# A new order of the beginning of an mLSTM with two feed-forward layers: scores among the broadcasts, and q and k of the third and fourth unit ahead of the first and second weight

## The chip, the cores and the metric

The kernel runs on one core of a Trainium2 chip. The metric is the device time of one execution in microseconds. The core's engines work side by side, each through its own list of instructions in order: TensorE (PE; its weight loads are shown as PEld), VectorE (DVE), ScalarE (ACT), GpSimd (POOL) and SyncE (SP), which here issues every transfer between DRAM and the core's memory. They wait for each other by semaphores.

## What is computed

A recurrent attention over 768 steps (batch 2, 8 heads, head dimension 40), and two feed-forward layers over its 1,536 tokens of width 320:

```python
for t in range(S):
    m_new = np.maximum(f_gate[:, :, t] + m, i_gate[:, :, t])
    f_stab = np.exp(f_gate[:, :, t] + m - m_new)
    i_stab = np.exp(i_gate[:, :, t] - m_new)
    m = m_new
    C = f_stab[:, :, None, None] * C + i_stab[:, :, None, None] * np.einsum('bhd,bhe->bhde', vt, kt)
    n = f_stab[:, :, None] * n + i_stab[:, :, None] * kt
    h_tilde = np.einsum('bhde,bhe->bhd', C, qt)
    denom = np.maximum(np.abs(np.einsum('bhd,bhd->bh', n, qt)[:, :, None]), 1.0)
    y[:, :, t] = h_tilde / denom / (1.0 + np.exp(-o_gate[:, :, t]))
h = np.maximum(np.maximum(x @ w1, x @ w2), x @ w3)     # 320 -> 768
x = h @ w_out                                          # 768 -> 320
h = x @ w_in                                           # 320 -> 2048
out = (h * np.tanh(softplus(h))) @ w_out2              # 2048 -> 320
```

## The kernel before

The recurrence is done in chunks of 128 steps. Six chunks times two batches make 12 units, numbered u0 to u11 in the code (u = 2 x chunk + batch); the "third and fourth unit" of the title are u2 and u3. Within a unit a step depends on the others through a 128 x 128 matrix of decays for each head, and on earlier chunks through a state. The first feed-forward layer runs in three blocks of 512 tokens (four units each), so its products (line 578) begin when u0 to u3 are through. Everything after that is products on TensorE, with the other engines converting weights and evicting results.

No scheduler decides the order. A text, PLAN, is read word by word, and each word calls a small function that records its instructions; each engine then runs what was recorded for it, in that order:

```python
def follow(plan):
    for word in plan.split():
        name, _, rest = word.partition(":")
        args, _, tags = rest.partition("@")
        act[name](*[int(a) if a.lstrip("-").isdigit() else a for a in args.split(",") if a], *[t for t in tags.split(",") if t])
```

The words of the beginning that are spoken of below, u being a unit:

- `first:n` loads the gates of the first chunk (fi0), of the others (fir), the identity (ident, into idt) or a mask. `ln:u` loads na (v, k and the output gate of a unit, 484 KB), `lq:u` q and k (line 300, two transfers), `l3:u` q in another layout, `lc:u` a broadcast cp, `fet:w,g` weight g of the first layer.
- `ma`, `fa`, `fe`, `fl`, `ia`, `ie` make the decays of the gates on VectorE, ScalarE and GpSimd; `pick` and `eye` make sel and idr from idt on ScalarE (lines 267 and 271).
- `F:u,j` broadcasts a row of decays over 128 partitions by four matmuls with sel (line 339); `D:u,j` scans it into half of the decay matrix dt on VectorE (line 346).
- `S:u` are the scores, q times k, eight matmuls (line 359); `X:u,j` multiplies them with dt on VectorE (line 365).
- `V:u` and `K:u` scale v and k by gates on GpSimd (lines 371, 381); `N:u` is the product of scores and v, with the state's part from u2 on (lines 398, 396); `den`, `sg`, `xn`, `xc` divide and gate; `T:u` transposes the result (line 429); `O`, `C`, `sd` bring the state forward.
- `sc`, `mg`, `rd`, `cut` convert a weight: two passes on ScalarE (lines 503, 504), a merge on VectorE (line 509), a split into two parts.
- `fill:n` are n matmuls on a cleared tile, whose result nobody reads:

```python
def _lq(u):
    for j in range(2):
        nc.sync.dma_start(qks[u % 2][64 * j:64 * j + D], qk2[u, j])
def _fill(n, tag):
    ps = bank(tag, f"fill{len(fills)}")
    fills.append(ps)
    for _ in range(n):
        nc.tensor.matmul(ps, warm[:, 0:P], warm, start=True, stop=True)
```

q and k have two buffers, so `lq:2` writes where u0's were and waits for `S:0`, and `lq:3` for `S:1`. na has two buffers as well; weights are fetched into three. All transfers stand in SP's one list, and SP waits in it: what is listed behind a waiting transfer is not issued.

Of the kernel before, what the change touches and what calls it, by code (L numbers as in the profile page):

```python
# [15 lines left out]
B, H, S, D = 2, 8, 768, 40  # L16
# [12 lines left out]
ZAT = (5, 12, 13)  # L29
LATE = {4: "i7", 6: "p4", 8: "p5", 10: "p6", 12: "p7"}  # L30
PLAN = (
# [882 lines left out]
```

## Time and profile before

| | us |
|---|---|
| three runs, median (lowest to highest) | 382.39 (374.51 to 383.19) |
| the profiled execution | 374.55 |
| its span, first to last instruction | 372.8 |
| TensorE busy in it | 367.4 |
| first products of the feed-forward layer start at | 33.31 |

Times in the rows are counted from the start of the span. A row of a timeline gives start, duration, engine, line, operation, out<-in and the shape, x the number of instructions merged into it, and in brackets the idle time before it with what ended it. A matmul's end is modelled, and some matmul records are missing (one of the 22 fills).

### The profile page before, as it was taken

The page shows a single profiled execution, that of the slowest core. Times are in us where ns is not written, and L with a number is a line of the kernel's source. Part 1 is how long each engine was busy: PE and PEld are TensorE (multiplying, and loading weights), DVE is VectorE, ACT ScalarE, POOL GpSimd, SP SyncE. Part 2 cuts the span into 40 slices and gives each one's busy share as a digit, 9 for nine tenths or more (in the row PEclk, how much of TensorE's full clock was granted, in tenths as well). Part 3 has the DMA queues.
Part 4 walks back from the last instruction along what each step waited for, and adds up shares of the span by engine and source line. Part 5 has one row for each costly group of instructions (what it writes and reads, how often), then busy time and mean ns, then how long its engine had stood idle before and what let it go on. Part 6 is the DMA issues. An engine that isn't in the chain of part 4 may idle for free.

```text
span 372.8 us, 7435 instructions
## 1 busy us (share of the span) xinstructions
PE 367.4 (99%) x2999; PEld 317.2 (85%) x3000; DVE 198.6 (53%) x344; ACT 175.5 (47%) x353; POOL 100.1 (27%) x111
## 2 busy tenths in 40 slices
PE   8999999999999999999999999999999999999996
PEld 4898888888888898888777889989989989989986
DVE  6989999998556853565581745512212112212112
ACT  4887777933413202555644876543333233333231
POOL 6784575755202022311540052330010110000000
PEclk9999999999999999999999999999999999999999
DMA  7879995938590310033220530000200000200001
GB/s 204 270 248 307 355 283 166 267 100 273 192 316 8 105 55 2 18 123 110 103 70 2 223 131 3 3 2 0 72 2 2 2 0 2 72 2 3 2 0 70
DMA packets 15668, 38.80 MB, mean 104 GB/s; under 512 B 1886, under 2 KB 8515, under 8 KB 15635
## 3 DMA queue, kind: packets, MB, share of 16 engines
q1 hardware_dynamic: 15635, 38.34, 31.3%
q8 instruction: 23, 0.38, 0.4%
q14 instruction: 10, 0.08, 0.1%
HBM read 36.29 MB, written 2.04 MB: 103 GB/s over the span
## 4 chain that ended last, share of the span: by engine, by line
PE 90%; DVE 3%; DMA 3%; ACT 1%; issue 1%; SPq 1%; DVEq 0%; ACTq 0%
PE mm L578 24%; PE o L719 23%; PE h L719 22%; PE it L398 4%; PE sc_c L359 2%; PE mz L621 2%; PE mz L620 2%; PE mz L622 2%; PE it L396 2%; DMA qall<-in_qk_dram 2%; PE mz L625 1%; PE mz L626 1%; PE sp L460 1%; DMA idt<-in_ident_dram 1%; PE xp L429 1%
## 5 line engine op out<-in xcount | busy, mean ns | idle before, releaser
L748 DVE TENSOR_TENSOR gl<-g,gh 128x512 fp32r<-128x512 f32 x48 | 34.8, 729 | 102.0 <-ACT g L747 102.0
L719 PE MATMUL o<-wo,gh 64*128 64x320 f32 (+1 forms) x736 | 85.0, 306 | 0.0
L719 PE MATMUL h<-zh,wi 64*128 64x512 f32 x480 | 75.2, 390 | 0.0
L578 PE MATMUL mm<-xh,w 128*128 128x512 f32 x270 | 72.0, 396 | 0.0
L719 PEld LDWEIGHTS o<-wo,gh 64*128 64x128 f32 (+1 forms) x736 | 65.1, 185 | 2.2 <-issue 0.4
L746 ACT ACTIVATE gh<-h 128x512 fp32r<-128x512 f32 x48 | 29.0, 604 | 77.8 <-PE h L719 77.6
L719 PE MATMUL o<-wo,gl 64*128 64x320 f32 (+1 forms) x368 | 59.3, 306 | 0.0
L578 PEld LDWEIGHTS mm<-xh,w 128*128 128x128 f32 x270 | 49.4, 188 | 10.7 <-issue 0.4
L719 PEld LDWEIGHTS h<-zh,wi 64*128 64x128 f32 x480 | 44.1, 185 | 9.3 <-ACT zraw L633 0.5
L719 PE MATMUL h<-zl,wi 64*128 64x512 f32 x240 | 47.3, 391 | 0.0
L578 PE MATMUL mm<-xl,w 128*128 128x512 f32 x162 | 45.7, 390 | 0.1
L578 PEld LDWEIGHTS mm<-xl,w 128*128 128x128 f32 x162 | 30.3, 188 | 6.9 <-issue 0.5
L719 PEld LDWEIGHTS o<-wo,gl 64*128 64x128 f32 (+1 forms) x368 | 36.1, 185 | 0.0
L596 DVE TENSOR_TENSOR zraw<-zraw,mm 128x512 f32<-128x512 f32 x36 | 24.6, 682 | 20.7 <-PE mm L578 19.1
L747 ACT ACTIVATE g<-h 128x512 f32<-128x512 f32 x48 | 29.2, 608 | 0.0
L719 PEld LDWEIGHTS h<-zl,wi 64*128 64x128 f32 x240 | 22.5, 184 | 5.3 <-issue 0.4
L658 POOL TENSOR_TENSOR zl<-zraw,zh 128x512 fp32r<-128x512 f32 x9 | 11.6, 1291 | 54.9 <-ACT zh L652 54.8
L606 POOL TENSOR_TENSOR hl<-zraw,hh 128x512 fp32r<-128x512 f32 x11 | 15.3, 1388 | 39.1 <-DVE hh L152 24.0
L398 PE MATMUL it<-vp,dt 128*128 128x41 f32 x192 | 25.2, 272 | 0.2 <-DVE dt L365 0.2
L398 PEld LDWEIGHTS it<-vp,dt 128*128 128x128 f32 x192 | 24.1, 192 | 0.5 <-DVE dt L365 0.3
L594 ACT ACTIVATE zraw<-mm 128x512 f32<-128x512 f32 x18 | 10.7, 592 | 21.8 <-PE mm L578 21.7
L346 DVE TENSOR_TENSOR_SCAN dt<-dt,eye 128x512 f32<-128x512 f32 x16 | 19.1, 1206 | 0.0
(153 smaller groups left out, 523.0 us busy)
## 6 DMA issues: line engine op xcount, KB each, us to landing
na<-in_nat_dram SPq DMA_DIRECT2D x12, 484.0 KB
raw_w<-in_w_dram SPq DMA_DIRECT2D x9, 640.0 KB
raw_i<-in_wi_dram SPq DMA_DIRECT2D x8, 640.0 KB
raw_p<-in_wo_dram SPq DMA_DIRECT2D x8, 640.0 KB
dt<-dram_f SPq DMA_DIRECT2D x8, 512.0 KB
qall<-in_qk_dram SPq DMA_DIRECT2D x24, 160.0 KB
raw_o<-in_wo_dram SPq DMA_DIRECT2D x3, 640.0 KB
out_dram<-ob SPq DMA_DIRECT2D x12, 160.0 KB
```

What stands on the lines that cost most here:

```text
L346: nc.vector.tensor_tensor_scan(half, *((t["fp", j], idr) if ("fp", j) in t else (half, eyes[0])), 0.0, op0=ALU.mult, op1=ALU.add)
L359: nc.tensor.matmul(scs[h % 2][:, (h // 2) * L:(h // 2 + 1) * L], qk[r:r + 64, 1, h // 2], qk[r:r + 64, 0, h // 2], start=True, stop=True)
L398: nc.tensor.matmul(it[:, h], t["dt"][:, h], vps[u % 2][:, h], start=(c == 0), stop=(c == 0 or h == h1 - 1))
L578: nc.tensor.matmul(ups[blk, m, i], *seq[k], start=(k == 0), stop=(k == 7))
L594: nc.scalar.activation(top(blk, m), ups[blk, m, 0], AF.Copy)
L596: nc.vector.tensor_tensor(top(blk, m), top(blk, m), ups[blk, m, i], op=ALU.max)
L606: engine(dve).tensor_tensor(ls, top(blk, m), h.bitcast(F32), op=ALU.subtract)
L658: nc.gpsimd.tensor_tensor(zl[:, j], zraw[:, j, t0:t0 + tb], zh[:, j].bitcast(F32), op=ALU.subtract)
L719: mm = nc.tensor.matmul(out_, a, r, start=first, stop=last).ins
L746: mark[blk, m] = nc.scalar.activation(gh, ps, AF.Mish)
L747: nc.scalar.activation(g, ps, AF.Mish)
L748: low[blk, m] = nc.vector.tensor_tensor(gl, g, gh.bitcast(F32), op=ALU.subtract)
```

## The change

The first lines of PLAN are written in another order. Nothing else differs: the same functions record the same work, but for ten fills fewer (22 to 12) and two table loads of ScalarE fewer (5 to 3), which follow from the order of exponentials and sigmoids. The first six lines of PLAN are new; from the seventh on the order is the same.

```diff
-    "tables: clear:4 first:0 clear:1 clear:2 clear:0 clear:3 fill:9@m1 first:1 clear:5 ln:0 first:2 lq:0 fet:w,0 ma:0 lq:1 l3:2 fa:0 fill:2@m0 ma:1 fe:0 fill:4@c1 "
...
+    "tables: clear:4 first:0 first:1 clear:1 clear:2 clear:0 clear:3 fill:8@m1 first:2 clear:5 clear:7 clear:6 lq:0 ln:0 ma:0 lq:1 ln:1 fa:0 ma:1 fe:0 "
+    "pick: eye: fa:1 ia:0 fl:0 fe:1 ie:0 F:0,1@m2 fill:2@m1 ma:2 ia:1 F:0,0@c0 ca:1 fl:1 D:0,1 out:1 flp:1 ie:1 F:1,1@m0 D:0,0 S:0@s0,s2 first:3 lq:2 l3:2 fet:w,0 fa:2 "
...
```

On SyncE, the transfers behind those of the gates (fi0, fir): na is v, k and o of a unit, qall q and k, raw_w a weight. Before:

```order
L305 DMA na0_132<-in_nat_dram 128x968
L186 DMA idt_86<-in_ident_dram 128x161
L300 DMA qall_93<-in_qk2_dram 40x1024 x2
L494 DMA raw_w0_137<-in_w13_dram 128x1280
L300 DMA qall_93<-in_qk2_dram 40x1024 x2
L310 DMA q32_143<-in_q3_dram 120x384
L294 DMA dram_c_104<-scr_105 16x128
L295 DMA dram_c_104<-scr_105 1x128
L305 DMA na1_206<-in_nat_dram 128x968
L186 DMA bmt_88<-in_bmask_dram 120x8
L494 DMA raw_w1_224<-in_w13_dram 128x1280
```

and now:

```order
L186 DMA idt_86<-in_ident_dram 128x161
L300 DMA qall_93<-in_qk2_dram 40x1024 x2
L305 DMA na0_139<-in_nat_dram 128x968
L300 DMA qall_93<-in_qk2_dram 40x1024 x2
L305 DMA na1_145<-in_nat_dram 128x968
L294 DMA dram_c_104<-scr_105 16x128
L295 DMA dram_c_104<-scr_105 1x128
L186 DMA bmt_88<-in_bmask_dram 120x8
L300 DMA qall_93<-in_qk2_dram 40x1024 x2
L310 DMA q32_203<-in_q3_dram 120x384
L494 DMA raw_w0_205<-in_w13_dram 128x1280
```

The identity moved ahead of na of u0, na of u1 came forward, and weight 0 moved behind q and k of u2 (the third qall).

Further down the same list, up to the third weight (raw_w2); cp is the broadcast of decays. Before:

```order
L300 DMA qall_93<-in_qk2_dram 40x1024 x2
L305 DMA na2_285<-in_nat_dram 128x968
L310 DMA q33_289<-in_q3_dram 120x384
L300 DMA qall_93<-in_qk2_dram 40x1024 x2
L330 DMA cp3_308<-dram_c_104 40x3x128 x3
L305 DMA na3_366<-in_nat_dram 128x968
L494 DMA raw_w2_372<-in_w13_dram 128x1280
```

and now:

```order
L300 DMA qall_93<-in_qk2_dram 40x1024 x2
L305 DMA na2_268<-in_nat_dram 128x968
L310 DMA q33_282<-in_q3_dram 120x384
L330 DMA cp3_291<-dram_c_104 40x3x128 x3
L494 DMA raw_w1_339<-in_w13_dram 128x1280
L305 DMA na3_356<-in_nat_dram 128x968
L494 DMA raw_w2_359<-in_w13_dram 128x1280
```

Weight 1 moved from ahead of this piece to just ahead of na of u3; na3 and raw_w2 keep the same set of transfers in front of them.

On TensorE, where the first fills end and the broadcasts (fp, of F) and scores (sc, of S) begin; gp are small transposes of gates. Before:

```order
L487 MATMUL fill2_153<-zraw_70 128x512
L252 MATMUL gp0_164<-idt_86,scr_105 128x16
L339 MATMUL fp0_1_174<-fzs_94,sel_95 128x128 x4
L339 MATMUL fp1_1_179<-fzs_94,sel_95 128x128 x4
L339 MATMUL fp0_0_185<-fzs_94,sel_95 128x128 x4
L339 MATMUL fp1_0_192<-fzs_94,sel_95 128x128 x4
L255 MATMUL gp1_208<-idt_86,scr_105 128x16
L359 MATMUL sc0_m2_214<-qall_93 128x128
L359 MATMUL sc0_s0_215<-qall_93 128x128
```

and now:

```order
L487 MATMUL fill0_121<-zraw_70 128x512
L339 MATMUL fp0_1_162<-fzs_94,sel_95 128x128 x4
L487 LDWEIGHTS zraw_70
L487 MATMUL fill1_167<-zraw_70 128x512
L487 LDWEIGHTS zraw_70
L487 MATMUL fill1_167<-zraw_70 128x512
L339 MATMUL fp0_0_172<-fzs_94,sel_95 128x128 x4
L339 MATMUL fp1_1_184<-fzs_94,sel_95 128x128 x4
L359 MATMUL sc0_s0_190<-qall_93 128x128
L359 MATMUL sc0_s2_191<-qall_93 128x128
```

The scores of u0 moved in between the broadcasts of u1; the first broadcast stands behind eight fills instead of 15 and a transpose.

## Rows read from the trace of the kernel before

**Rows 1.** The page: span, and busy time, share and instructions of each engine.
```profile
span 372.8 us, 7435 instructions
...
PE 367.4 (99%) x2999; PEld 317.2 (85%) x3000; DVE 198.6 (53%) x344; ACT 175.5 (47%) x353; POOL 100.1 (27%) x111
```

**Rows 2.** Waits of TensorE up to 130 us: total us, times, longest.
```profile
PE it L398 <- DVE dt L365: 0.2, 1, 0.2
PE sc_c L359 <- DMA qall<-in_qk_dram: 0.2, 1, 0.2
```

**Rows 3.** Timeline of TensorE, from the first fill to the first products.
```profile
1.39 6.11 PE L487 MATMUL fill<-zraw 128*128 128x512 bf16 x15 [1.39 <-DVE zraw L162]
...
7.74 2.00 PE L339 MATMUL fp<-fzs,sel 128*128 128x128 f32 x16
...
11.26 1.55 PE L339 MATMUL fp<-fzr,sel 128*128 128x128 f32 x12
...
13.83 1.68 PE L487 MATMUL fill<-zraw 128*128 128x512 bf16 x6
15.36 1.87 PE L398 MATMUL it<-vp,dt 128*128 128x41 f32 x16
...
27.40 0.76 PE L398 MATMUL it<-vp,dt 128*128 128x41 f32 x6
...
29.56 0.53 PE L429 MATMUL xp<-idt,xn 128*128 128x128 f32 x3
...
33.31 1.41 PE L578 MATMUL mm<-xh,w 128*128 128x512 f32 x5
```

**Rows 4.** Timeline of VectorE, up to the scores of u0.
```profile
2.49 0.47 DVE L191 TENSOR_TENSOR_SCAN scr<-scr 16x128 f32<-16x128 f32 x1
...
4.36 0.35 DVE L222 TENSOR_TENSOR fzs<-scr,fzs 16x128 fp32r<-16x128 f32 x1
...
8.51 4.57 DVE L346 TENSOR_TENSOR_SCAN dt<-fp,idr 128x512 f32<-128x512 f32 x4 [1.14 <-PE fp L339]
...
14.31 0.68 DVE L365 TENSOR_TENSOR dt<-sc_s,dt 128x512 f32<-128x512 f32 x1
```

**Rows 5.** Timeline of ScalarE, the same stretch and behind it.
```profile
5.97 0.21 ACT L267 ACTIVATE sel<-idt 128x16 fp32r<-128x16 f32 x1 [1.31 <-DMA idt<-in_ident_dram]
...
15.60 1.28 ACT L215 ACT_TABLE_LOAD   x1
...
26.96 0.80 ACT L503 ACTIVATE dec_w<-raw_w 128x640 f32<-128x640 f32 x1 [0.33 <-DMA raw_w<-in_w_dram]
...
28.33 0.25 ACT L154 ACTIVATE xn<-xn 128x64 f32<-128x64 f32 x1
```

**Rows 6.** Windows of 10 us: length, busy time of each engine, granted clock, transfers' share, GB/s.
```profile
0.00:10.00 10.00, 8.51 (x34) 4.36 (x35) 6.75 (x16) 4.01 (x12) 6.71 (x17) 1.00 0.73 207
10.00:20.00 10.00, 9.95 (x98) 8.70 (x99) 9.93 (x15) 8.93 (x22) 7.15 (x10) 1.00 0.85 263
20.00:30.00 10.00, 9.84 (x90) 9.21 (x88) 8.54 (x19) 8.12 (x19) 6.59 (x7) 1.00 0.81 252
...
40.00:50.00 10.00, 10.00 (x59) 8.16 (x58) 9.47 (x13) 7.47 (x17) 6.80 (x11) 1.00 1.01 321
```

**Rows 7.** Transfers on the page: issues, KB each.
```profile
na<-in_nat_dram SPq DMA_DIRECT2D x12, 484.0 KB
raw_w<-in_w_dram SPq DMA_DIRECT2D x9, 640.0 KB
...
qall<-in_qk_dram SPq DMA_DIRECT2D x24, 160.0 KB
```

**Rows 8.** Timeline of SyncE: first issues.
```profile
0.74 0.40 SPq L186 DMA_DIRECT2D scr<-in_fi_dram  x1
...
1.65 0.41 SPq L305 DMA_DIRECT2D na<-in_nat_dram  x1
```

**Rows 9.** Timeline of GpSimd: V of u3.
```profile
25.74 0.73 POOL L371 TENSOR_TENSOR vp<-na,gTr 128x328 f32<-128x328 f32 x1
```

9 rows, old and new, of the table PLAN are left out of this document.

## The prediction

> **What bounds the kernel now.** I read the page first, for the engines' shares, then the waits of TensorE, then its timeline, then the timelines of the engines that feed it, and last the transfers in windows of 10 us. TensorE is busy 367.4 of 372.8 us [rows 1]. Before 130 us it waits for the cleared tile at the start (1.39 us) and twice for 0.2 us [rows 2, 3]. So the time is the length of TensorE's stream, and what the beginning is worth is its padding and the waiting that the padding hides. The padding is the fills: 15 from 1.39 us, over 6.11 us, and seven (six were recorded) from 13.83 us to 15.36, where N of u0 begins [rows 3]. They stand there because other work is late. The first F at 7.74 needs sel, which ScalarE made only at 5.97, after waiting 1.31 us for idt; N of u0 needs the X of VectorE, which ran to 14.31 + 0.68 = 14.99 [rows 3 to 5].
>
> The second thing to see is the transfers. In the windows from 10 to 30 us their engines are busy 0.85 and 0.81 of the time, at 263 and 252 GB/s [rows 6]. One queue, SP's, feeds them in the order of the program, so what lands at 25 us is a question of how many bytes stand in front of it.
>
> **The change, part by part.** *The start of F.* The ident transfer now stands ahead of na of u0. That takes 484 KB (495.6 kB) out of its way, 1.9 us at 263 GB/s [rows 6, 7], and one issue of 0.41 us [rows 8]. sel can then be made from about 3.7 to 4.1 us, and two other things come last: fzs, ready at 4.36 + 0.35 = 4.71 [rows 4], and the eight fills that are left, at 6.11 / 15 = 0.41 us each [rows 3]: 1.39 + 8 x 0.42 = 4.8. So F starts at 4.8 in place of 7.74, 2.9 us earlier. The scans D start 0.77 us behind F now (8.51 against 7.74); four take 4.57, the two X 0.6 to 0.68 each [rows 4]. With F at half clock they start 1.3 behind. X of u0 ends near 4.8 + (0.8 to 1.3) + 4.57 + 1.28 = 11.5 to 12.0, against 14.99: N of u0 comes about 3 us earlier if its operands are there, and the seven fills ahead of it have no use any more; two stand behind the first F, two ahead of S of u2. (22 fills become 12.)
>
> *What moves at no cost.* Two of five table loads of ScalarE vanish; the one at 15.60 takes 1.28 us [rows 5]. TensorE waits for ScalarE nowhere there [rows 2], so I count nothing; without that cover they would be worth 2.6 us. Weight 0 is fetched behind q and k of u2. It is wanted by the products at 33.31 [rows 3]; by its place (3.0 MB in front of its end, 2.07 by 10 us and 0.263 a us from there) it would land before 16 us, with its conversion, three operations of about 0.8 us, long before 33 (the first of weight 2's takes 0.80 [rows 5]). q and k of u2 and u3 land earlier: today's lateness costs 0.2 us, once [rows 2]; that is their whole direct gain.
>
> *The new wait on the queue.* q and k of u2 go into the buffer of u0, so their issue waits until the scores S of u0 are done. Behind it on SP stand q3, weight 0, cp and all that follows; in the old order weight 0 stood ahead of such a wait and kept the engines busy. Ahead of it there are now 16 + 80 + 80.5 + 320 + 484 + 320 + 484 + 12 = 1,797 KB = 1.84 MB (q and k of a unit are two of 160 KB [rows 7]). The first 10 us move 2.07 MB [rows 6], so these are through at 10 - (2.07 - 1.84) / 0.26 = 9.1 us. S of u0 ends at 4.8 + 1.9 (three F of 2.00 / 4 each, two fills) + 1.5 (S of u0 lies between 9.74 and 11.26 today) = 8.2 if TensorE runs at its full clock, at 11.6 at half of it, near 9.2 if the clock rises at about 7 as today [rows 3]. Issue to use of a small transfer takes 1.75 us (fi is issued at 0.74, its scan runs at 2.49 [rows 4, 8]). So the transfer engines run dry for 0.8 to 4.2 us less what today's idle share (0.15 of 10 us, 1.5 us) already holds: from nothing to 2.7 us later. I take 1.0 us, nearer the case of a clock that rises as today (9.2 + 1.75 - 9.1 = 1.8, less half of the 1.5).
>
> *Where the gain stops.* na of u3 and weight 2 have exactly the same transfers in front of them in both orders, only shuffled: 5,405 KB = 5.53 MB ahead of na. By the windows (4.70 MB by 20 us, then 252 GB/s [rows 6]) they begin at 20 + 0.83 / 0.252 = 23.3 us and weight 2, behind na, ends at 20 + (0.83 + 0.50 + 0.66) / 0.252 = 27.9 (na of 484 KB, a weight of 640 KB [rows 7]); ScalarE, which waits for weight 2, starts on it at 26.96 [rows 5]. The bytes so give the place to within 1 us, and the shares leave at most 0.15 x 10 + 0.19 x 5 = 2.4 us of idle to be won before 25. What hangs on these two: V of u3 at 25.74, over 0.73 [rows 9], then N of u3, whose part with V is at 27.40 [rows 3]; and on ScalarE, behind weight 2's conversions, the small copy of u1's xn at 28.33 [rows 5], which the transpose of u1 (29.56 to 30.09 [rows 3]) needs. With landings as today, N of u3 could start at 25.74 + 0.73 = 26.5, 0.9 us earlier. With landings 1.0 us later, the copy runs from 29.3 to 29.6 and the transpose ends near 29.8 in place of 30.09: 0.3 us earlier. With landings 2.7 us later 1.4 us are lost; with landings 2.4 us earlier up to 2.4 are won. From there the chain to the products (33.31) is the same work.
>
> *Behind it.* From 40 to 50 us TensorE is busy 10.00 of 10 us, transfers are at 1.01 and VectorE at 9.47 [rows 6]. A start 0.5 us earlier can be lost there to a weight that lands no sooner: bounds 0 and the whole of it. I keep it, since TensorE waits for nothing in that stretch.
>
> **Sum.** Between 0.3 and 0.9 us I take 0.5: the profiled execution took 374.55 us (span 372.8 [rows 1] and 1.75 around it), so 374.0. The median of the three runs shown is 382.39 (374.51 to 383.19): the profiled execution lies with the lowest of them, and what made the other two longer is not in its rows.
>
> **TensorE's clock.** The window rows call the granted clock 1.00 from the start [rows 6]. But fills of 512 columns come 0.41 us apart over the first 6.11 us, which is the 1.2 GHz level, and 0.22 apart from 13.83 to 15.36, the 2.4 GHz level [rows 3]. Ahead of the rise there were fills without a gap from 1.39. In the new order there are eight, then short matmuls. The Trainium skill ("TensorE: Matmul & The Clock Gate", Part 1) says that the throttled level is the default and that activity releases it; the fills at 0.41 us agree, and by that rule taking away seven of them speaks against this change, where the rows only show that the rise came after this many. By the rows the sum stays at 374.0; by the rule, if the rise came as late as 20 us, it would be the 377.7 of the first rival, which is worked out from rows.
>
> **The rivals.** *The clock stays low (the other side).* F, S and N of the beginning then run at half speed up to a time t. The new order has done (t - 4.8) / 2 of the work by then, the old one t - 7.74 - 1.5 (its second fills). They are equal at t = 13.7; below that nothing is lost by it. At t = 20 it is 3.2 us: 377.7. Slower by 2% (7.5 us) takes t = 29. For it: only eight fills before the short matmuls. Against it: F follows them at once. 0.08, of which 0.02 beyond 2%.
>
> *The queue gives back its idle time.* S is early, the engines don't run dry, landings come up to 2.4 us earlier: 374.55 - 2.4 = 372.2. For it the shares of 0.85 and 0.81 [rows 6]; against it the new wait on SP. 0.10.
>
> *The queue runs dry for longer.* 2.7 us later, 1.4 lost, 376.0; a stall beyond that has no price here. 0.06, of which 0.02 beyond 2%.
>
> *Transfers are slower than in the profile.* They are near full from 4 to 50 us and more, so some 15% more time per byte costs about 7 to 8 us; that would make the 382.39 and 383.19 among the three. Then both orders wait for the same bytes, and the changed kernel reads about 382 as well: the change doesn't do what it says, and compared like with like it is no change. 0.22.
>
> *The longer runs go*, since q and k no longer stand behind weights: 374 where the median was 382, faster by over 2%. Only the one wait of 0.2 us speaks for it [rows 2]. 0.04.
>
> **How the numbers follow.** The forecast, 0 to 1.2 us won (373.3 to 374.6), has 0.50; the rivals hold the rest. About 2% is what a measurement of this kernel can tell from no change. Faster by that: the last rival alone, 0.04. Slower: 0.02 of the clock and 0.02 of the dry queue, 0.04. Within: 0.92. The range must take in the slow transfers at 0.22, and so the clock at t = 20; below, part of the early landings is left out: 372.6 to 383.0. The likeliest case by itself is 373.3 to 374.6.
>
> **What would show it.** F at about 4.8 us and D at 5.6 to 6.1: the start is right. N of u0 near 12.5. Then a wait of GpSimd's V or of TensorE for na of u3 around 25 to 26 us, and the first products between 32.3 and 33.1. If they start at 31, the queue gave its idle time. If F and S take twice their length until 14 us and more, it was the clock. I am wrong if something other than the transfers of 23 to 28 us holds N and the transposes, or if F can't start at 4.8.

## The result, and the profile after

The changed kernel took 378.09 us (median of six, 376.79 to 379.19), the kernel before 378.52 beside it (374.24 to 383.19). Compared without the long executions of the kernel before, the ratio is 1.0091 [1.0062, 1.0121]: slower by about 3.4 us. That is less than 2%, and on the other side of zero from the forecast of 374.0. The two medians can only be read with one thing known: executions of the kernel before come at about 375 us and at about 382.5, and the comparison leaves the second kind out (the section on the clock says what goes with it).

The page of the changed kernel, as [rows 1]:

```profile
span 375.0 us, 7410 instructions
...
PE 368.7 (98%) x2990; PEld 319.8 (85%) x2990; DVE 199.1 (53%) x344; ACT 173.0 (46%) x351; POOL 101.1 (27%) x111
```

The span grew by 2.2 us. TensorE issues ten fills fewer (one record was missing before) and is busy 1.3 us longer. Its waits from 3 to 42 us, as [rows 2]:

```profile
PE sc_s L359 <- DVE dt L346: 0.6, 1, 0.6
PE xp L429 <- DVE xn L418: 0.3, 1, 0.3
PE it L398 <- POOL vp L371: 0.2, 1, 0.2
PE fp L339 <- DVE fzs L222: 0.2, 1, 0.2
```

Waits of 1.3 us in all cannot turn a lead of 2 us into a loss of 2.2. Its timeline, as [rows 3], shows where the lead goes:

```profile
1.39 3.26 PE L487 MATMUL fill<-zraw 128*128 128x512 bf16 x8 [1.39 <-DVE zraw L162]
4.88 0.63 PE L339 MATMUL fp<-fzs,sel 128*128 128x128 f32 x4 [0.23 <-DVE fzs L222]
5.35 0.61 PE L487 MATMUL fill<-zraw 128*128 128x512 bf16 x2
...
11.29 0.58 PE L359 MATMUL sc_s<-qall 64*128 64x128 f32 x1 [0.58 <-DVE dt L346]
...
13.29 3.63 PE L398 MATMUL it<-vp,dt 128*128 128x41 f32 x16
...
18.85 1.08 PE L487 MATMUL fill<-zraw 128*128 128x512 bf16 x2
...
22.33 1.88 PE L398 MATMUL it<-vp,dt 128*128 128x41 f32 x16
...
35.65 1.45 PE L578 MATMUL mm<-xh,w 128*128 128x512 f32 x5
```

F starts at 4.88 instead of 7.74. N of u0 starts at 13.29 instead of 15.36, 2.07 us early. Its sixteen multiplications then take 3.63 us; those of u1, at 22.33, take 1.88, as those of u0 took 1.87 before [rows 3]. N of u1, which comes 2.30 late, stood here in the kernel before:

```profile
20.03 1.98 PE L398 MATMUL it<-vp,dt 128*128 128x41 f32 x16
```

The products at 35.65 are 2.34 late. Everything is lost between 13.3 and 22.3 us. The windows of 10 us, as [rows 6], and two of 2 us within them:

```profile
0.00:10.00 10.00, 8.38 (x55) 5.73 (x56) 8.64 (x17) 4.93 (x15) 8.72 (x18) 1.00 0.69 190
10.00:20.00 10.00, 9.42 (x49) 8.09 (x48) 7.73 (x14) 6.07 (x15) 5.04 (x7) 0.55 0.91 252
20.00:30.00 10.00, 9.76 (x93) 9.16 (x93) 7.15 (x14) 6.29 (x17) 6.89 (x9) 0.94 0.75 236
```

```profile
10.00:12.00 2.00, 1.42 (x11) 1.15 (x12) 2.00 (x4) 1.92 (x6) 2.00 (x4) 0.75 1.02 264
...
20.00:22.00 2.00, 2.00 (x19) 1.88 (x20) 1.43 (x3) 0.00 (x0) 0.69 (x1) 0.69 1.06 240
```

The granted clock, the third number from the end, is 0.55 from 10 to 20 us where it was 1.00 [rows 6]. In the windows of 2 us it is 0.75 at 10 to 12, 0.50 in each of the four to 20, and 0.69 at 20 to 22: TensorE ran at 1.2 GHz from about 11 to about 21 us. The clock had risen early (two fills take 0.61 at 5.35, the 2.4 GHz rate). So it did not come up late; it came up and fell again. Ahead of the fall stood multiplications of 64x128 and 128x128 with no fill since 5.96, and the one wait of 0.58 us, from 10.71 to 11.29. A mean of 0.75 from 10 to 12 puts the fall at 11.0, inside that wait and only 0.3 us after its start.

GpSimd, for V of u3 [rows 9]:

```profile
21.31 0.74 POOL L371 TENSOR_TENSOR vp<-na,gTr 128x328 f32<-128x328 f32 x1 [1.92 <-DMA na<-in_nat_dram]
23.69 0.45 POOL L551 TENSOR_TENSOR w<-dec_w,w 64x128 fp32r<-64x128 f32 x1 [1.64 <-ACT w L154]
24.22 0.45 POOL L552 TENSOR_TENSOR w<-dec_w,w 64x128 fp32r<-64x128 f32 x1
...
25.43 1.27 POOL L549 TENSOR_TENSOR w<-dec_w,w 128x512 fp32r<-128x512 f32 x1
26.65 1.00 POOL L376 TENSOR_TENSOR cb<-cp,q 120x384 f32<-120x384 f32 x1
27.61 1.73 POOL L371 TENSOR_TENSOR vp<-na,gTr 128x328 f32<-128x328 f32 x1
```

The order has a second effect here. Three cuts of weight 0 (0.45, 0.45, 1.27) now stand between V of u2 and cb of u3, which is the broadcast cp times q (line 376) and which the state's part of N needs. In the kernel before only the long one stood between them; the two short ones lay ahead of V of u2:

```profile
16.20 0.45 POOL L551 TENSOR_TENSOR w<-dec_w,w 64x128 fp32r<-64x128 f32 x1
16.72 0.45 POOL L552 TENSOR_TENSOR w<-dec_w,w 64x128 fp32r<-64x128 f32 x1
...
23.90 1.88 POOL L376 TENSOR_TENSOR cb<-cp,q 120x384 f32<-120x384 f32 x1 [0.55 <-DMA cp<-dram_c]
```

cb of u3 is 2.75 us late (26.65 against 23.90), but the first cut itself waited 1.64 us for ScalarE, so not all of that is the cuts' place. V of u3 follows cb without a wait for na. On SyncE, na of u3 was issued at 18.77 us (18.85 before) and weight 2 at 19.17 (20.57 before): neither was issued late.

### The profile page after: what moved, and what is told of

It is laid out like the page before. It is cut to its first block, busy times and chain, and to the rows that moved or that the text cites. A ratio compares the mean times of both kernels' runs of the same rounds, so it can differ in the third digit from the quotient of the medians.

```text
span 375.0 us, 7410 instructions
## 1 busy us (share of the span) xinstructions
PE 368.7 (98%) x2990; PEld 319.8 (85%) x2990; DVE 199.1 (53%) x344; ACT 173.0 (46%) x351; POOL 101.1 (27%) x111
## 4 chain that ended last, share of the span: by engine, by line
PE 89%; DVE 6%; POOL 1%; issue 1%; ACT 1%; DVEq 0%; POOLq 0%; ACTq 0%
PE mm L578 24%; PE o L719 23%; PE h L719 22%; PE it L398 4%; PE mz L622 2%; PE mz L621 2%; PE mz L620 2%; PE sc_c L359 2%; PE sp L460 1%; PE it L396 1%; DVE dt L346 1%; PE mz L625 1%; PE mz L626 1%; PE sc_s L359 1%; PE xp L429 1%
## 5 line engine op out<-in xcount | busy, mean ns | idle before, releaser
L398 PE MATMUL it<-vp,dt 128*128 128x41 f32 x192 | 26.9, 284 | 0.4 <-POOL vp L371 0.2
L398 PEld LDWEIGHTS it<-vp,dt 128*128 128x128 f32 x192 | 25.7, 203 | 0.9 <-POOL vp L371 0.4
```

The lines of the kernel that those rows point to most:

```text
L398: nc.tensor.matmul(it[:, h], t["dt"][:, h], vps[u % 2][:, h], start=(c == 0), stop=(c == 0 or h == h1 - 1))
```

## Experiments: fills put back

Two theories were to be told apart: the clock, and the transfers (na of u3 and weight 2, issued in the new order, cost it whatever the clock). Fills write a bank (a part of the memory that takes TensorE's results) that nobody reads then; fill:4@c0 is four of them. Each execution has a mean granted clock; I call the clock held where that is 0.998 or more. This says that the clock was not seen to fall. It does not see a clock that comes up late (last section).

**Four ahead of S of u1**

```diff
-S:1@m0,s1
+fill:4@c0 S:1@m0,s1
```

> The changed order with four fills (512 columns each, 0.22 us apart at the full clock) put ahead of S of u1, where TensorE stood still for 0.58 us at 10.7. Clock theory: what cost the changed order its lead is the granted clock of 0.50 from 12 to 20 us, which followed a stretch of short multiplications with that pause; with the pause filled the clock stays at 1.00, N of u0 starts at 13.3 to 13.8 and takes 1.9 us instead of 3.63, the products start at 32.3 to 33.3 instead of 35.65, and the time is 373.5 to 374.8 us. Transfer theory: the later na of u3 and weight 2 cost it whatever the clock; the products start at 35 or later and the time stays at 376.8 to 379.2.

Measured: 376.97 to 379.63 us in four executions, the clock at 0.982 to 0.989. The clock stayed at 1.00 past 11 us, but the price was only put off. Waits of TensorE, then windows of 2 us:

```profile
PE it L398 <- POOL vp L371: 1.0, 1, 1.0
```

```profile
22.00:24.00 2.00, 1.01 (x9) 0.70 (x6) 0.70 (x2) 1.19 (x4) 1.03 (x2) 1.00 1.00 372
24.00:26.00 2.00, 2.00 (x12) 2.00 (x11) 1.97 (x3) 0.67 (x2) 1.85 (x4) 0.51 0.92 334
```

Running early, TensorE now waits 1.0 us for V, and behind that wait the clock is at 0.51. It is back only between 36 and 38 us (0.58).

**Eight: four more ahead of the first gate transpose**

```diff
-gt:0@c1
+fill:4@c1 gt:0@c1
```

> The run with four fills ahead of S of u1, and four more ahead of the first transpose of the gates (7.8 us), where TensorE is ahead of the scans of D on VectorE, so that they should delay no D. Clock theory: the clock stays at 1.00 to 30 us at least as surely as with four, products at 32.3 to 33.3, 373.5 to 374.8 us; if four were too few and the clock still fell there, this one tells whether it is the amount of dense work. Transfer theory: 376.8 to 379.2 as without fills.

Measured: 374.38, 374.42 and 374.43 us with the clock held, and one of 380.38. In the profile the clock is 1.00 throughout and the span 372.6:

```profile
14.40 1.98 PE L398 MATMUL it<-vp,dt 128*128 128x41 f32 x16
...
26.96 0.86 PE L398 MATMUL it<-vp,dt 128*128 128x41 f32 x6 [0.45 <-POOL vp L371]
...
33.20 1.40 PE L578 MATMUL mm<-xh,w 128*128 128x512 f32 x5
```

The loss is gone with the transfers left as changed, in three of four executions. So is the gain: N of u0 leads by 1.0 us, the V part of N of u3 by 0.44 and the products by 0.11 (14.40, 26.96, 33.20 against 15.36, 27.40, 33.31 [rows 3]).

**The same kernel in more executions**

> The run with eight added fills once more, in more rounds, for the size of what is left of the change once the clock is held. Its products started at 33.20 against 33.31 of the kernel before and its span was 372.6 against 372.8. Clock theory: 374.4 us and a ratio of 0.998 to 1.000 to the kernel before, with a granted clock of 0.998 to 1.000 in those executions. Transfer theory: its one earlier comparison was lucky, and the ratio is that of the changed kernel, 1.006 to 1.012.

Measured: 376.06 median of twelve (374.24 to 379.06), ratio 1.0046 [1.0007, 1.0085]. The clock held in two of twelve (374.56 and 374.98). The expectation of a held clock failed: the first four had been lucky. Two executions in which the clock was not held are as fast (374.24 at 0.995, 375.04 at 0.995), so a short fall need not show in the time. In this profile, TensorE's waits, GpSimd, and windows:

```profile
PE it L396 <- POOL cb L376: 1.7, 1, 1.7
...
```

```profile
25.16 1.92 POOL L376 TENSOR_TENSOR cb<-cp,q 120x384 f32<-120x384 f32 x1
```

```profile
26.00:28.00 2.00, 0.67 (x4) 0.48 (x4) 0.81 (x4) 1.27 (x4) 2.00 (x3) 1.00 0.65 222
...
30.00:32.00 2.00, 2.00 (x12) 1.67 (x12) 1.33 (x6) 0.52 (x3) 0.00 (x0) 0.50 0.52 185
```

cb of u3 begins on GpSimd at 25.16 and takes 1.92; TensorE waits 1.7 us for it, and 2 us after that wait the clock falls (29.2). In the profile of the same kernel above, where the clock held, cb came earlier:

```profile
24.30 1.00 POOL L376 TENSOR_TENSOR cb<-cp,q 120x384 f32<-120x384 f32 x1
```

**Four ahead of the gates only**

> The changed order with only the four fills ahead of the first transpose of the gates (at 7.8 us), and the 0.58 us pause of S of u1 as it is. Two readings of the clock theory stand against each other. If the pause at 10.7 us brought the clock down, it falls at about 11 again and the time is 376.8 to 379.2 us. If it was the long row of short multiplications without dense work between them, four fills keep the clock past 11 us; it may fall later, as it did at 24 with four fills ahead of S of u1, and the time is 374.4 us where it holds and 376.5 to 379 where it doesn't.

Measured: 377.63 median (373.98 to 379.86), ratio 1.0066 [1.0022, 1.0109], held in none of ten. The clock stayed up past 11 us and fell at 27.2, during a wait of 1.8 us for cb of u3 that began at 25.6. The two readings were not told apart: the fills delayed S of u1, and the pause was gone with them.

**The pause taken away without a fill**

```diff
-S:1@m0,s1
+S:1@m0,c0
```

> The changed order without any added fill, but half of S of u1 goes to a bank that D has already left, so that the 0.58 us pause at 10.7 us is gone by itself. If the pause brought the clock down at 11 us, the clock now holds past 12 and N of u0 starts at about 12.0 to 12.6 and takes 1.9 to 2.0 us; it may still fall behind a later wait, and the time is 374.0 to 377. If it was the stretch of short multiplications without dense work, the clock falls at about 11 again, N of u0 takes about 3.6 us, and the time is 376.3 to 379.2 as in the changed kernel.

Measured: 378.05 median of four (377.72 to 378.48), ratio 1.0090 [1.0066, 1.0115]. The 0.58 us did not vanish: it moved to N of u0, which now waited for X. The clock held past 12 and fell behind that wait (0.63 at 14 to 16 us, 0.51 at 16 to 18), rose, and fell again at 28 behind 0.90 us of wait for cb. N of u0 began at 11.93. Neither expectation fits whole: short multiplications without fills did not bring the clock down at 11, and a pause goes ahead of each fall, but no fill stood shortly ahead of the first fall either, so the two stay unseparated.

**Fills taken out of the kernel before**

```diff
-S:1@m0,s1 fill:7@c0 G:1
+S:1@m0,s1 G:1
```

> The kernel before without its seven fills at 13.83 us (between S of u1 and N of u0). Clock theory: without dense work in that place the clock of the old order falls too, a granted clock near 0.5 shows for several us somewhere between 14 and 30 us, and the products start 1 to 3 us later than 33.31: 376 to 378 us against 374.3. Transfer theory: the fills are read by nobody and N of u0 can start up to 1.5 us earlier; the clock stays, and the time is 373.5 to 374.5.

Measured: 376.60 median of four, three at 376.37 to 376.67 with the clock at 0.989 to 0.995, one at 385.33 with 0.964. The clock held in none. The one profile is of the long execution: in the place of the fills TensorE waits 1.2 us for X of u0, and behind that wait the clock falls at 16.2 us. The three others are 1.5 to 1.8 us above the median of the kernel before with a held clock (374.88). But that kernel loses its clock in 53 of 100 executions with its fills, so four of four without them are too few to show that it needs them.

## Experiments: the transfers

**Old order of transfers, all else changed.** Behind ident, SyncE's queue is as before.

```diff
-lq:0 ln:0 ma:0 lq:1 ln:1
+lq:0 ln:0 fet:w,0 ma:0 lq:1 l3:2
...
-first:3 lq:2 l3:2 fet:w,0
+first:3 fet:w,1
```

> The changed order on all engines but SyncE's queue, where everything behind ident (weight 0 and 1, na of u1 and u3, q and k of u2 and u3) is issued in the old order. Clock theory: TensorE does the same as in the changed kernel, its clock falls at about 11 us to 0.50 and the time is 376.8 to 379.2. Transfer theory: na of u3 and weight 2 land up to 1.4 us earlier, products at 33.5 to 34.5, and the time is 374 to 375.5 although the clock falls.

Measured: 376.89 to 377.50 in three of four executions, with the clock at 0.986, and 383.21 with 0.978. Old transfers do not give the time back. The one profile is of the long execution, and it is not what the clock theory expected: here the clock rose later, S of u1 never stood still for D, and the clock stayed at 1.00 through S of u1 and N of u0 without an added fill. It passed two waits of 1.05 and 0.62 us for q and k of u2 as well, behind two fills, and fell at 24.1, at the end of a wait of 1.5 us for those of u3. So the old order of transfers brings waits of its own.

**Old order of transfers with eight fills**

> The changed order with the eight added fills of the run before, and SyncE's queue back in the old order behind ident. With the clock held at 1.00 by the fills, what is left between this and the run with eight fills alone (374.4 us, products at 33.20) is the order of transfers. Clock theory: the same volume stands ahead of na of u3 in both, so 374.0 to 374.8 us and products at 32.8 to 33.4. Transfer theory in its small form (the new order loses up to 0.8 us at na of u3 even at full clock, V of u3 25.74 before and 0.45 us of wait at N of u3 with eight fills): products at 32.3 to 32.7 and 373.4 to 373.8 us. If q and k of u2 come late, S of u2 waits, and the clock may fall there again: 377 us and more.

Measured: 375.92 median of ten, ratio 1.0034 [1.0006, 1.0061]; the clock held in seven (374.56 to 376.36, median 375.67). The profile:

```profile
PE sc_s L359 <- DMA qall<-in_qk_dram: 1.6, 1, 1.6
```

S of u2 waits 1.6 us for q and k, and the clock stays at 0.999 of full all the same. So a wait of that length does not always bring it down. And at a held clock the old order of transfers is no better than the new (374.4 to 375.0 in five of the six such executions of the kernel with eight fills, 380.38 in the sixth). That the transfers cost the changed kernel its time whatever the clock is refuted, by the eight fills above and by this run. The small form of the theory, up to 0.8 us at na of u3, gets no support: V of u3 started at 26.13, later than the 25.27 with the new transfers, behind cb on GpSimd and not for na. But the new wait for q and k stands in the way of a clean comparison.

**na of u3 ahead of weight 1, one cut of weight 0 behind V of u3** (with eight fills; the first step of weight 2 on ScalarE also moves back, which the excerpt leaves out)

```diff
-K:1 lc:3
+K:1 lc:3 ln:3
...
-K:2 cut:w,0,0 S:3@s2,c0
+K:2 S:3@s2,c0
...
-sg:1 l3:4
+sg:1 cut:w,0,0 l3:4
```

> The changed order with eight added fills; na of u3 is issued ahead of weight 1 instead of behind it, the second cut of weight 0 stands behind V of u3 on GpSimd instead of ahead of it, and the first step of weight 2 on ScalarE goes behind the sigmoid of u3. With the clock held, what comes late is V of u3 (0.45 us of wait at N of u3, na landing at 25.1). Both theories: V of u3 starts about 1.2 us earlier (24.1 instead of 25.27), N of u3 does not wait, products at 32.5 to 32.8 instead of 33.20, 373.7 to 374.1 us while the clock is at 1.00. If weight 1 or 2 now comes late, its cuts stand ahead of the second group of products and the gain is lost: 374.4 or more.

Measured: 376.78 median of twelve, ratio 1.0052 [1.0013, 1.0091]. The one execution with a held clock took 373.37; in the other eleven it fell (0.985 to 0.994). Without the move, the kernel with eight fills held its clock in two of twelve beside it, so the move neither held the clock nor can be said to have lost it.

## Experiments: the clock

**More fills where TensorE waits.** To the eight, two ahead of S of u3 and two ahead of N of u3:

```diff
-S:3@s2,c0
+fill:2@m2 S:3@s2,c0
...
-N:3@s2
+fill:2@m2 N:3@s2
```

> The changed order with eight added fills, and two more ahead of S of u3 (21.85 us) and two ahead of N of u3, where TensorE waited 0.45 us for V of u3 with eight fills (and 1.0 us with four, where the clock then fell at 24 us). Clock theory: at the full clock the four cost 0 to 0.9 us of TensorE and some of it lies in that wait, so 374.4 to 375.2 us with granted clock 1.00 in each execution. If the count of fills matters little once the clock is up, it is no faster than with eight. Transfer theory has no use for them: no change of the 376.8 to 379.2 of the changed kernel, which the run with eight fills already speaks against.

Measured: 376.18 median of ten, 1.0035 [0.9993, 1.0077]; held in four (373.46 to 375.42). A clock of 1.00 in each execution had been expected. In the profile it fell at 29.5, behind waits of 0.43 and 0.21 us, the first of them straight behind two of the fills.

**The same four in the kernel before**

> The kernel before with two fills ahead of S of u3 and two ahead of N of u3, where TensorE waits for q, k and V when transfers come late. Clock theory: at the full clock it takes 374.3 to 375.2 us (up to 0.9 us of fills, part of it in waits), and fewer of its executions lie at 382 than the eight of thirteen of the kernel before. Transfer theory: the same two times as the kernel before, no rarer at 382.

Measured: 375.50 median, 1.0022 [0.9984, 1.0059]; held in eight of ten (374.75 to 376.87), against 15 of 25 executions of the kernel before beside them: too few to call it rarer.

**The kernel before, for its clock**

> The kernel before, unchanged, for its granted clock. Its executions lay at 374.2 to 375.3 us and at 381.6 to 383.2 us, with mean granted clocks of 1.00 in the first and 0.976 to 0.982 in the second. Clock theory: wherever a profile shows the longer time, the granted clock falls to 0.50 between 14 and 42 us, behind a stretch in which TensorE waited or did short work; where it shows the shorter, the clock stays at 1.00 from 7 us. Transfer theory: the longer time comes with transfers that take longer, and with a clock like that of the shorter.

Measured: 374.13 and 375.38 with a clock of 1.00, 382.51 and 383.70 with 0.978 and 0.976. The profile fell on the first kind, so where the clock falls in the others was not seen.

**All cuts of weight 0 behind K of u3** (eight fills, na of u3 ahead of weight 1, the steps of weight 2 behind the halves of u3; the excerpt shows the cuts)

```diff
-lq:4 cut:w,0,1 G:2
+lq:4 G:2
...
-K:3 N:3@s2
+K:3 cut:w,0,1 cut:w,0,0 N:3@s2
```

> The changed order with eight added fills; on GpSimd the three cuts of weight 0 (0.45, 0.45 and 1.27 us) go behind K of u3 instead of standing between V of u2 and V of u3; the steps of weight 2 on ScalarE and VectorE go behind the halves of u3, and na of u3 is issued ahead of weight 1. Cut theory: what made TensorE wait 1.7 to 1.8 us for cb of u3 with eight and with four fills is this work on GpSimd (cb of u3 began at 25.2 to 26.4, in the kernel before at 23.9), and that wait brought the clock down at 27 to 29. Then cb of u3 begins at 23.3 to 24, V of u3 at 24.3 to 25, TensorE waits under 0.6 us at N of u3, more of the executions keep a granted clock of 0.998 and more, and those take 373.2 to 374.2 us. Transfer theory: na and cp of u3 land late themselves, the wait stays over 1 us and the clock falls as often: 376 to 378 us.

Measured: 375.44 to 376.73, the clock at 0.990 to 0.995, held in none of four. In the profile:

```profile
24.31 1.00 POOL L376 TENSOR_TENSOR cb<-cp,q 120x384 f32<-120x384 f32 x1 [0.70 <-DMA cp<-dram_c]
```

cb of u3 now waits 0.70 us for cp itself. It began 0.85 us earlier than in the second profile with eight fills (25.16), and TensorE's waits shrank from 1.9 to 0.9 us. But in the first profile of that kernel cb began at 24.30 with the cuts in their old place and TensorE waited 0.4 us for V, so what the cuts cost is not shown: two profiles of one kernel differ by as much. The clock fell all the same:

```profile
28.00:30.00 2.00, 2.00 (x19) 1.77 (x18) 2.00 (x5) 1.82 (x6) 1.79 (x3) 0.93 0.82 244
30.00:32.00 2.00, 2.00 (x12) 1.96 (x12) 1.72 (x6) 1.02 (x3) 1.98 (x2) 0.50 0.40 163
```

**The same with five more fills**

```diff
-S:3@s2,c0
+fill:2@m2 S:3@s2,c0
...
-N:3@s2
+fill:3@m2 N:3@s2
```

> The run with eight fills and late cuts, with two more fills ahead of S of u3 and three ahead of N of u3 (1.1 us of TensorE at the full clock, in the lead that TensorE has there). If waits bring the clock down, these fills stand in what is left of them: clock at 0.998 to 1.00 in most executions, 373.5 to 374.8 us. If the clock falls wherever short multiplications run long enough, it falls as often as with eight: 376 to 378.

Measured: 375.20 to 375.95, the clock held in five of five. Same windows:

```profile
28.00:30.00 2.00, 2.00 (x19) 1.87 (x18) 1.42 (x4) 1.04 (x5) 1.85 (x3) 1.00 0.85 236
30.00:32.00 2.00, 1.93 (x18) 1.52 (x16) 1.76 (x6) 1.13 (x3) 1.42 (x2) 1.00 0.61 216
```

Five fills are all the difference: none of four against five of five, side by side, where the kernel before held in one of nine. What it lost elsewhere is one new wait:

```profile
PE mm L578 <- DVE st L480: 1.3, 1, 1.3
```

**That wait taken away**, with the state update of u3 ahead of the steps of weight 2 on VectorE, and its scaling on ScalarE likewise (the place of the update in the thirteen-fill kernel, then here):

```diff
-xl:3,1 mg:w,2 sd:3 cut:w,1,1,1 P:0,0,0 cut:w,1,0 rd:w,2,1 P:0,0,1 C:3
+xl:3,1 C:3 cut:w,1,1,1 cut:w,1,0 mg:w,2 P:0,0,0 rd:w,2,1 P:0,0,1
```

> The run with thirteen fills and late cuts, with the state update of u3 on VectorE put ahead of the steps of weight 2 there (and its scaling on ScalarE likewise), because the third group of products waited 1.3 us for it (at 37.25). If fills hold the clock and that wait was what the late cuts cost, the wait is gone: 374.0 to 374.9 us, granted clock 0.998 and more in most executions. If weight 1 or 2 then comes late instead, a wait of like size shows between 36 and 42 us and the time stays at 375.2 to 376.

Measured: 375.16 median, 1.0010 [0.9989, 1.0032]; held in twelve of twelve. The wait went, and another of 0.8 us came at 39 us (for a bank that ScalarE empties later): 0.8 of the 1.3 us came back in another place.

**The wait filled with eight fills**, added to the eight from above, cuts and transfers as in the changed kernel:

```diff
-N:3@s2
+fill:8@m2 N:3@s2
```

> The changed order with eight added fills and eight more ahead of N of u3 (1.8 us), where TensorE waited 1.7 us for cb of u3; GpSimd and the transfers are left as they are. If the wait itself brought the clock down, it now stays at 1.00 and N of u3 starts when it did with eight (27.1 to 27.5): 374.4 to 375.2 us in most executions. If the clock goes down for another reason, a granted clock of 0.50 still shows behind 27 us and the time stays at 376 to 378.

> The run with sixteen fills (four, four, and eight ahead of N of u3) once more, for its time in more executions: three of five lay at 374.1 to 375.0 with a clock of 1.00. If dense work in the place of the wait holds the clock, more than half of the executions lie at 374.0 to 375.2; if those three were luck, most lie at 376 to 378 as with eight.

Measured: 374.13, 374.30, 374.95, 376.64 and 384.74 in the first five, 375.37 median in the twelve of the second, ratio 1.0023 [0.9994, 1.0052]; held in fifteen of seventeen, against six of sixteen without the eight (the kernel before held in 14 of 32 beside the first and in 14 of 36 beside the second). One of the fifteen is the 384.74, where the clock came up late, and one of the six the 380.38. From the second profile:

```profile
5.39 0.61 PE L487 MATMUL fill<-zraw 128*128 128x512 bf16 x2
...
13.34 1.98 PE L398 MATMUL it<-vp,dt 128*128 128x41 f32 x16
...
18.62 1.88 PE L398 MATMUL it<-vp,dt 128*128 128x41 f32 x16
...
25.08 1.89 PE L487 MATMUL fill<-zraw 128*128 128x512 bf16 x8
26.80 0.38 PE L396 MATMUL it<-st,cb 120*128 120x123 f32 x2
27.02 0.80 PE L398 MATMUL it<-vp,dt 128*128 128x41 f32 x6
...
33.20 1.42 PE L578 MATMUL mm<-xh,w 128*128 128x512 f32 x5
```

This is the changed order with the clock up. From N of u0 (13.34) to N of u1 (18.62) are 5.28 us; in the changed kernel, from the same start (13.29), 9.04. TensorE waits for nothing in either stretch. The difference, 3.8 us, is what the fall cost, and it is more than the whole result. N of u1 leads the kernel before by 1.4 us (20.03); then the fills stand where TensorE had waited, because cb of u3 ends at 26.2, and at the V part of N of u3 the lead is 0.38 (27.40 [rows 3]).

## The clock over all executions

| kernel | executions | clock held | median while held, us | all, us |
|---|---|---|---|---|
| before | 100 | 47 | 374.88 | 373.56 to 384.95 |
| before without seven fills | 4 | 0 | | 376.37 to 385.33 |
| before with four more | 10 | 8 | 375.36 | 374.75 to 381.41 |
| changed | 6 | 0 | | 376.79 to 379.19 |
| changed, eight fills | 16 | 6 | 374.50 | 374.24 to 380.38 |
| changed, sixteen fills | 17 | 15 | 375.03 | 374.11 to 384.74 |
| changed, late cuts, eight fills | 4 | 0 | | 375.44 to 376.73 |
| changed, late cuts, thirteen (two kernels) | 17 | 17 | 375.57 | 374.23 to 381.68 |

The 53 executions of the kernel before in which the clock was not held report 0.971 to 0.995 and take 376.38 to 384.95, 382.68 in the middle. I had put the 382 of the first runs down to slow transfers. Of the hundred, all above 377 us show the lower clock, and none below 376. The size fits too, by an estimate from these numbers: a mean clock of 0.978 over 381 us is 8.4 us of full-speed clock missing, and those executions take 7.8 us longer (382.68 against 374.88). So the clock goes with the long executions and is enough to explain them, though no profile shows the place. In the changed order with fewer than eight added fills, with either order of transfers, the clock held in none of 28 executions.

While the clock is held, the new order is worth nothing that these runs can tell: 374.5 to 375.6 in the middle, against 374.9. Nor is the changed kernel slower than an average execution of the kernel before: its six have a mean of 377.9 us, the hundred one of 379.0. It is slower than those in which the clock held. What the versions with thirteen fills have ahead of both kernels is the steadiness: by the reported clock it held in 17 of 17 executions, the mean of which is 375.8 us, though one of them took 381.68.

Two things stay open. The first is what exactly brings the clock down. Ahead of the falls in the profiles stand waits among short multiplications, the longest of each between 0.4 and 1.8 us. The clock fell as early as 0.3 us after the start of such a wait (changed kernel) and as late as 2.7 us after the end of one (late cuts with eight fills). Other waits passed without a fall: 1.6 us with the old transfers and eight fills, and 1.3 and 0.8 us among the products of the two kernels with thirteen. And the same kernel holds the clock in one execution and not in the next. The Trainium skill ("TensorE: Matmul & The Clock Gate", "Why this matters for your kernels") says to leave no long gaps between bursts of matmuls, since the clock falls back behind them. The gaps that it names are longer than any wait seen ahead of a fall here (1.8 us at most), so the traces differ from it: shorter waits stood ahead of falls. The Trainium skill ("TensorE: Matmul & The Clock Gate", Part 1) also says that one and the same kernel runs a different number of matmuls at the low clock at its start from one execution to the next. The kernel with sixteen fills agrees: in one profile two fills at 5.39 us already run at the 2.4 GHz rate, in the other the clock came up only between 26 and 29 us. The second thing open is whether the long executions at a reported clock of 0.999 to 1.00 (380.38, 381.68, 384.74) have one cause; only the last was profiled (below).

## Why the prediction was wrong, step by step

- *The start of F*: right. 4.88 against 4.8, held by fzs as said.
- *D and X*: 0.6 to 1.1 us too early. D started at 6.66, not at 5.6 to 6.1; VectorE had two scans of the later units ahead of it (1.38 us from 4.76 and 0.46 from 6.17). N of u0 at 13.29 instead of 12.5 comes from S of u1, which waited 0.58 us for D and then ran at half clock; where it did neither, N of u0 began at 11.93.
- *The new wait on the queue*: no cost. q and k of u2 were issued at 7.91, not after 9.2, since the clock rose ahead of 5.35 and not at 7. The term "1.0 us later" was zero there; it had been priced with the clock of the old order.
- *Fills at no cost*: the step that failed. The sum took the removed fills for padding whose only use was to pass the time until operands come, and the rival asked only how late the clock would rise (equal "at t = 13.7; below that nothing is lost by it"). The clock rose early, before 5.35, and fell again at 11.0 for 10 us; no sentence of the prediction has a fall. Between N of u0 and N of u1 that cost 3.8 us (9.04 against 5.28), more than the forecast gain. Fills put back hold the clock more often, and thirteen against eight did so with nothing else changed. Whether the missing fills or the wait at 10.71 brought this fall about stays open. The rival's price (377.7 for half clock up to 20 us) is near what was measured (376.8 to 379.2), but it had a chance of 0.08, a lowered clock came six times in six, and the price comes from another course of the clock: that they agree is luck.
- *Where the gain stops*: the place was right, the cause only in part. With the clock up, the lead does end at cb and V of u3. In the first profile with eight fills cb of u3 starts straight behind the last cut of weight 0 on GpSimd, and V of u3 behind cb; neither waits for a landing there. "What moves at no cost" followed weight 0 only to the products at 33 and not to the queue in which its cuts stand. With the cuts moved, cb waited for the landing of cp instead, and what the cuts cost by themselves is not shown.
- *The gain of 0.5 us*: not to be seen. In the two versions whose clock held most often the ratios are 1.0010 [0.9989, 1.0032] and 1.0023 [0.9994, 1.0052].
- *Slow transfers as the cause of 382*: nothing speaks for it; those executions report a lower clock, which is enough for their length (estimate above).

## What to carry to other kernels

Count a filler matmul as work that may have a product: the clock. Before taking fillers out, or before moving short matmuls forward to a place where they will wait, price the stretch behind it at half rate; where waits can't be avoided, fill them. And follow a delayed operand through every engine's queue to what stands behind it, not only to its own consumer.

## What was not expected of the hardware

In these profiles the column for the granted clock reads 1.00 until the first change of an execution, at either rate. In the profiled execution of 384.74 us it is 1.00 everywhere, but:

```profile
10.40 1.89 PE L487 MATMUL fill<-zraw 128*128 128x512 bf16 x4
...
20.33 3.63 PE L398 MATMUL it<-vp,dt 128*128 128x41 f32 x16
...
25.89 1.08 PE L487 MATMUL fill<-zraw 128*128 128x512 bf16 x2
29.16 1.88 PE L398 MATMUL it<-vp,dt 128*128 128x41 f32 x16
```

Four fills take as long as eight do at 25.08 in the profile of the same kernel above, and N of u0 takes 3.63 us: the clock did not rise until between 26 and 29 us. That is the late rise of the first rival, in one execution of seventeen of the kernel with sixteen added fills. And the clock fell where TensorE had hardly been idle: in the changed kernel it is busy 2.00 of 2.00 us from 8 to 10 us and up to 10.71, and the clock is down at 11.0:

```profile
8.00:10.00 2.00, 2.00 (x17) 1.90 (x17) 2.00 (x2) 0.88 (x4) 1.92 (x3) 1.00 0.80 223
```
